# An attention-then-MLP kernel on one core: the prologue's u, first cumulative products and zero products rewritten, and the last tile in halves

## The chip, the core and the metric

The kernel runs on one core of a Trainium2 chip. The time is device time in microseconds (us) of one execution, from outside the span; the profiled span is from the first to the last instruction. TensorE is called PE (its weight loads PEld), VectorE DVE, ScalarE ACT, GpSimd POOL and SyncE SP. SPq and ACTq are the queues from which SP and ACT issue DMAs. Every engine takes its instructions in the order in which the program gives them.

## What is computed

A linear attention with a decaying state, for 4 batches of 8 heads, 768 steps and 48 dimensions, then an MLP with a leaky ReLU over the 3072 rows of 384:

```python
state = 0
for t in range(S):
    cur = u * k[t] (outer) v[t]
    y[t] = r[t] @ (state + cur)
    state = w[t] * state + k[t] (outer) v[t]
x = y, heads side by side            # 3072 x 384
h = x @ w_in                         # 384 x 2048
out = max(0.01 * h, h) @ w_out       # 2048 x 384
```

All inputs and the output are float32; the matrix products run in bf16 with float32 accumulation.

## The kernel before

**Attention by chunks.** The 3072 rows are 24 chunks of 128 steps (6 for each batch). In a chunk the decay is brought into r and k by cumulative sums of log w, so that the chunk needs only matrix products. The steps of chunk i, with engine and line:

- log of w (ACT, L254; for the first four chunks in pairs, L258);
- cum, cumulative sums of the logs by a product with a triangle of ones, and their column sums (PE, L282 and L284; for chunks 0 to 3 L268 and L274, and a second product cum2 at L293 in place of DVE's neg, L300);
- exp and exn, exponentials of the sums and their negatives (ACT, L307 and L310);
- kr = k and r times these (DVE, L314);
- trans, the transposes of kr (PE, L346) and a copy to rkT (ACT L351 or DVE L353); from chunk 10 on a DMA transpose from SP's queue instead (L357);
- scores "at" (PE, L367), two masks (DVE, L375), the mix "y" of state and scores with v (PE, L386 and L392), the new state: kv (PE, L405), tt (DVE, L413), st (POOL, L423);
- the part of u: t1 = r times u (POOL, L318), t2 = t1 times k (POOL, L322), diag, its sum over a head (DVE, L333), vsc = v times diag (POOL, L337), and ysb = y + vsc (DVE, L400);
- ytr, the transposes of ysb (PE, L433) and the copy into xT (ACT, L441); from chunk 18 on by DMA from SP's queue (L436).

**u.** It is loaded as one row by ACT's queue (L204), spread over 128 partitions by a float32 product with a row of ones (PE, L208) and copied to `ukb` (DVE, L211), which t1 reads.

**MLP by tiles.** The rows are also cut in tiles of 256 or 128 (L446). For a tile PE makes the hidden products "hp" (L462), ACT the leaky ReLU into "gt" (L468), PE the output products "op" (L474), ACT the copy to "osb" (L481), and ACT's queue the store (L485). hp of a tile needs xT of its chunks and the weights `w_in`, op needs gt and `w_out`; the weights come in four quarters each, cast to bf16 by DVE (L239 and L242). gt has two buffers, so hp of tile q waits for op of tile q-2.

**Loads.** All come from SP's queue in one list (L507): chunk 0, 1, 2, `w_in` quarters among chunk 3, chunk 4, then the four quarters of `w_out`, then the other chunks.

**Order.** Class Order plans the program ahead: every step has an engine, an assumed duration, what it needs, what PSUM buffers it takes (pool "att" has 5, pool "mlp" 3) and a rank. Again and again it takes the step that can start first by the plan; at equal times the one with the lower rank, which is the chunk's number plus an offset from OFF (L495), or above 100 for MLP products. A DMA that waits for a result (transposes, in the same SP queue as the loads) is taken ahead of a load only if the plan has it ready earlier by SLACK (L497). The program is emitted in that order. While the planned time is under WARM (L494), gaps of PE in the plan are filled with products of zeros (L609), of 512 columns, as many as the planned gap holds.

Of the kernel before, what the change touches and what calls it, by code (L numbers as in the profile page):

```python
# [15 lines left out]
class Order:  # L16
# [20 lines left out]
    def run(self, pools):  # L37
        ends, out = {}, []
        self.times = []
        free = {}  # L40
        slots = {p: [None] * n for p, n in pools.items()}
        place = {}
        todo = {}
# [64 lines left out]
def kernel(  # L108
# [47 lines left out]
    lwp_b = [const.tile([128, 2, H, 64], BF16, name=f"lwp{i}") for i in range(EARLY // 2)]  # L156
    one_row = const.tile([1, 128], F32, name="one_row")
    u_row = const.tile([1, DM], F32, name="u_row")
    kr_b = [const.tile([128, 2 * H, 64], BF16, name=f"kr{i}") for i in range(NB3)]
# [6 lines left out]
    def constants():  # L166
        for t, x, op in ((tri2, 1.0, ALU.is_gt), (trin2, -1.0, ALU.is_ge)):
            nc.gpsimd.memset(t[:], x)
            nc.gpsimd.affine_select(
                out=t[:], in_=t[:], compare_op=op, fill=0.0, base=0, pattern=[[-1, 2], [1, 256]],  # L170
                channel_multiplier=-2,
            )
        nc.gpsimd.memset(tri[:], 1.0)
        nc.gpsimd.affine_select(
            out=tri[:], in_=tri[:], compare_op=ALU.is_gt, fill=0.0, base=0,
            pattern=[[1, 128]], channel_multiplier=-1,
        )
        make_identity(nc, ident)
        nc.vector.memset(ones[:], 1.0)
        nc.vector.memset(idle[:], 0.0)  # L180
        nc.vector.memset(one_row[:], 1.0)
        for t in lwp_b:
            nc.vector.memset(t[:, :, :, D:64], 0.0)
        for t in kr_b + lw_b:
            nc.vector.memset(t[:, :, D:64], 0.0)
        for t in st_b:
            nc.vector.memset(t[:], 0.0)
# [15 lines left out]
    def load_u():  # L203
        nc.scalar.dma_start(out=u_row[:], in_=u.rearrange("h d -> (h d)").rearrange("(a n) -> a n", a=1))  # L204

    def spread_u():
        ub = stage["u"] = ps_att.tile([128, DM], F32, name="ub", tag="att")
        nc.tensor.matmul(ub[:], lhsT=one_row[:], rhs=u_row[:], start=True, stop=True)  # L208

# [53 lines left out]
    def a_cum(i):  # L263
        if i < EARLY:
            r0, m = 64 * (i % 2), i // 2
            cum = att[i]["cum"] = ps_att.tile([128, 512], F32, name="cum", tag="att")
            for j in range(2):
                nc.tensor.matmul(  # L268
                    cum[:, 0:DM], lhsT=tri2[r0 : r0 + 64, j, 2 * r0 : 2 * r0 + 128],
                    rhs=lwp_b[m][r0 : r0 + 64, j, :, 0:D], start=(j == 0), stop=False, skip_group_check=True,  # L270
                )
            for p in range(NP):
                for j in range(2):
                    nc.tensor.matmul(  # L274
                        cum[:, DM + p : DM + p + 1], lhsT=pair(lwp_b[m][r0 : r0 + 64, j], p),
                        rhs=ones[r0 : r0 + 64, :], start=False, stop=(p == NP - 1 and j == 1),
                        skip_group_check=True,
                    )
# [3 lines left out]
        nc.tensor.matmul(cum[:, 0:DM], lhsT=tri[:], rhs=lw[:, :, 0:D], start=True, stop=False, skip_group_check=True)  # L282
        for p in range(NP):
            nc.tensor.matmul(  # L284
                cum[:, DM + p : DM + p + 1], lhsT=pair(lw, p), rhs=ones[:], start=False, stop=(p == NP - 1),
                skip_group_check=True,
            )

    def a_cum2(i):
        cum2 = att[i]["neg"] = ps_mlp.tile([128, H, D], F32, name="cum2", tag="mlp")  # L290
        r0, m = 64 * (i % 2), i // 2
        for j in range(2):
            nc.tensor.matmul(  # L293
                cum2[:], lhsT=trin2[r0 : r0 + 64, j, 2 * r0 : 2 * r0 + 128],
                rhs=lwp_b[m][r0 : r0 + 64, j, :, 0:D], start=(j == 0), stop=(j == 1),
            )
# [148 lines left out]

    sizes = [256, 256, 128, 128, 128, 128, 256, 256, 256, 128, 256, 128, 256, 256, 256]  # L446
    assert sum(sizes) == B * S
# [30 lines left out]

    def m_copy(q, ts):
        osb = osbs[q, ts] = opool.tile([128, NOUT], F32, name="osb")  # L480
        nc.scalar.copy(out=osb[:], in_=ops.pop((q, ts))[:])  # L481

    def m_store(q, ts):
        row = starts[q] + ts * 128
        nc.scalar.dma_start(out=out[row : row + 128, :], in_=osbs.pop((q, ts))[:])  # L485

# [15 lines left out]
    add("const", "POOL", 3.2, constants, rank=-1)  # L502
    add("u", "ACT", 0.3, load_u, lag=2.4, rank=-3)
    add("ub", "PE", 1.2, spread_u, lag=0.2, rank=-3, needs=["u"], takes=(("att", ("ukb",)),))
    add("ukb", "DVE", 0.5, copy_u, needs=["ub"], rank=-3)
    users = []
    queue = [('in', 0), ('in', 1), ('in', 2), ('w_in', 0), ('in', 3), ('w_in', 1), ('w_in', 2), ('w_in', 3), ('in', 4), ('w_out', 0), ('w_out', 1), ('w_out', 2), ('w_out', 3)] + [("in", i) for i in range(5, NCH)]  # L507
    for kind, n in queue:
        past_user = users[-NIN:][:1] if len(users) >= NIN else []
        if kind == "in":  # L510
            if n < EARLY:
                order.alias(("w", n), ("wp", n // 2))
                if n % 2 == 0:
                    add(("wp", n // 2), "DMA", 1.35, load_wp, n // 2, lag=1.95,
                        needs=[("logp", n // 2 - 1)] if n else [])
                    add(("logp", n // 2), "ACT", 0.86, a_logp, n // 2, needs=[("wp", n // 2)], rank=n)
# [64 lines left out]
    for q, mb in enumerate(sizes):  # L581
# [8 lines left out]
        for ts in range(mb // L):  # L590
            for part in range(NQ):
# [4 lines left out]
            tiles.append((q, ts))  # L596
            add(("copy", q, ts), "ACT", 0.48, m_copy, q, ts, rank=0, needs=[("out", q, ts, NQ - 1)]
                + [("store", *x) for x in tiles[-NOUTB - 1 : -NOUTB]])
            add(("issue", q, ts), "ACT", 0.3, m_store, q, ts, rank=-1, needs=[("copy", q, ts)])
# [43 lines left out]
```

## Time and profile before

| what | value |
|---|---|
| median of 7 runs (lowest, highest) | 187.23 us (186.68, 189.46) |
| the profiled execution: time, span | 187.73 us, 186.0 us |
| PE busy | 176.5 us (95%), 1954 products |
| DVE, ACT, POOL busy | 113.3, 113.0, 109.2 us (59 to 61%) |
| PE hp L462, op L474 busy | 72.1 us, 69.5 us |
| zero products L609 | 22, 7.5 us, all before 17 us |
| moved by DMA | 34.46 MB, 115553 of 120696 packets under 512 B |
| granted PE clock in the record | 1.00 throughout |

The slices of the page cut the span in 40 parts; a digit is the busy share in tenths. The chain of waits follows the work that ended last back from the last instruction, at each step to what released it. A line of the timeline has start and length in us, engine, line, what is written and read, and in brackets how long the engine had been idle and for whom. PE's products are pipelined: the ends are modelled, so that sums of busy time are above the pure streaming time.

### The profile page before, as it was taken

What the parts mean: (1) busy time and instruction counts of PE and PEld (TensorE: products, weight loads), DVE (VectorE), ACT (ScalarE), POOL (GpSimd) and SP (SyncE); (2) the same over time, 40 slices, a digit from 0 to 9 for tenths busy, and PEclk for the clock granted to TensorE, in tenths of its full rate; (3) what the DMA queues carried; (4) which work ended last, traced back from release to release, by engine and by line L of the source; (5) the groups of instructions that cost most, each with busy time, mean ns of one, the idle gap of its engine ahead of it and who ended that gap; (6) DMA issues with size and microseconds to landing.
All of it is one profiled execution on the core that took longest, in us unless ns stands there. A gap on an engine that the chain in (4) does not pass through costs nothing.

```text
span 186.0 us, 4892 instructions
## 1 busy us (share of the span) xinstructions
PE 176.5 (95%) x1954; PEld 134.0 (72%) x1955; DVE 113.3 (61%) x187; ACT 113.0 (61%) x218; POOL 109.2 (59%) x144
## 2 busy tenths in 40 slices
PE   7999767999999999999999999999999999999992
PEld 1365557956878878678796688869785786887961
DVE  4377994296689988838395675857575474460000
ACT  2666657914757857577694468669573465662731
POOL 7579954504666699996748786656558368320000
PEclk9999999999999999999999999999999999999999
DMA  6999899999989999999979999899997989422102
GB/s 134 186 211 276 221 351 175 335 375 165 272 164 230 187 202 185 201 184 225 208 154 176 187 197 207 170 193 201 183 161 155 184 173 216 111 63 64 45 6 79
DMA packets 120696, 34.46 MB, mean 185 GB/s; under 512 B 115553, under 2 KB 118626, under 8 KB 120674
## 3 DMA queue, kind: packets, MB, share of 16 engines
q1 hardware_dynamic: 117216, 29.43, 81.8%
q10 hardware_dynamic: 3458, 4.72, 7.5%
q8 instruction: 15, 0.25, 0.6%
q14 instruction: 7, 0.06, 0.1%
HBM read 25.17 MB, written 4.72 MB: 161 GB/s over the span
## 4 chain that ended last, share of the span: by engine, by line
PE 73%; SPq 11%; DMA 9%; DVE 2%; ACT 2%; issue 1%; ACTq 0%; DVEq 0%
PE op L474 33%; PE hp L462 26%; SPq L201 9%; DMA ws<-in_moe_w_out_dram 4%; PE at L367 3%; DMA rkT<-kr 3%; SPq L225 2%; DMA wp<-in_w_dram 2%; PE y L392 2%; PE cum L282 2%; PE trp L346 2%; PE ytr L433 2%; PE y L386 1%; PE kv L405 1%; PE cum L284 1%
## 5 line engine op out<-in xcount | busy, mean ns | idle before, releaser
L462 PE MATMUL hp<-xT,w_in_b 128*128 128x256 bf16 (+1 forms) x720 | 72.1, 252 | 0.5 <-ACT xT L441 0.2
L474 PE MATMUL op<-w_out_b,gt 128*128 128x384 bf16 x384 | 69.5, 326 | 0.3 <-DVE w_out_b L242 0.3
L468 ACT ACTIVATE gt<-hp 128x512 bf16<-128x512 f32 x96 | 56.7, 596 | 21.1 <-PE hp L462 17.5
L462 PEld LDWEIGHTS <-w_in_b 128*128 128x128 bf16 x720 | 62.8, 114 | 3.9 <-DVE w_in_b L239 0.9
L474 PEld LDWEIGHTS <-gt 128*128 128x128 bf16 x384 | 35.6, 98 | 20.6 <-DVE w_out_b L242 0.5
L318 POOL TENSOR_TENSOR t<-in,ukb 128x384 f32<-128x384 f32 x24 | 24.2, 1009 | 22.7 <-DMA in<-in_r_dram 22.4
L375 DVE TENSOR_TENSOR mt<-at,tri 128x512 bf16<-128x512 f32 x48 | 30.9, 684 | 9.8 <-PE at L367 9.6
L314 DVE TENSOR_TENSOR kr<-e,in 128x768 bf16<-128x768 f32 x24 | 27.3, 1139 | 10.9 <-ACT e L310 9.7
L423 POOL TENSOR_TENSOR st<-tt,e 48x192 bf16<-48x192 f32 x40 | 22.6, 565 | 14.1 <-DVE tt L413 10.3
L337 POOL TENSOR_TENSOR vsc<-in,diag 128x384 f32<-128x384 f32 x24 | 22.7, 946 | 11.0 <-DVE diag L333 10.5
L322 POOL TENSOR_TENSOR t<-t,in 128x384 f32<-128x384 f32 x24 | 26.0, 1082 | 2.1 <-DMA in<-in_k_dram 0.8
L400 DVE TENSOR_TENSOR ysb<-y,vsc 128x384 bf16<-128x384 f32 x24 | 13.3, 552 | 11.9 <-PE y L392 8.0
L307 ACT ACTIVATE e<-cum 128x388 f32<-128x388 f32 x24 | 11.9, 494 | 13.7 <-PE cum L284 5.4
L481 ACT COPY osb<-op 128x384 f32<-128x384 f32 x24 | 11.4, 476 | 14.2 <-PE op L474 14.0
L300 DVE SCALAR_TENSOR_TENSOR neg<-cum,lw 128x384 f32<-128x384 f32 x20 | 11.1, 553 | 9.9 <-ACT e L307 9.7
L333 DVE TENSOR_REDUCE diag<-t 128x8 f32<-128x384 f32 x24 | 13.1, 545 | 5.2 <-POOL t L322 5.2
L329 POOL CAST vb<-in 128x384 bf16<-128x384 f32 x20 | 12.3, 616 | 5.4 <-DMA in<-in_v_dram 3.7
L254 ACT ACTIVATE lw<-in 128x384 bf16<-128x384 f32 x20 | 10.4, 520 | 8.1 <-DMA in<-in_w_dram 8.1
L310 ACT ACTIVATE e<-neg 128x384 f32<-128x384 f32 x20 | 10.4, 522 | 4.4 <-DVE neg L300 2.6
L441 ACT COPY xT<-ytr 128x384 bf16<-128x384 bf16 x18 | 8.6, 477 | 2.1 <-ACT osb L481 1.2
L367 PE MATMUL at<-rkT 48*128 48x128 bf16 x192 | 9.5, 219 | 0.3 <-DMA rkT<-kr 0.3
L413 DVE TENSOR_TENSOR tt<-kv,st 128x384 f32<-128x384 f32 x16 | 8.8, 550 | 0.9 <-PE kv L405 0.6
(55 smaller groups left out, 135.9 us busy)
## 6 DMA issues: line engine op xcount, KB each, us to landing
in<-in_r_dram SPq DMA_DIRECT2D x24, 192.0 KB, 4.6
in<-in_k_dram SPq DMA_DIRECT2D x24, 192.0 KB, 4.8
in<-in_v_dram SPq DMA_DIRECT2D x24, 192.0 KB, 4.8
out_dram<-osb ACTq DMA_DIRECT2D x24, 192.0 KB, 3.1
in<-in_w_dram SPq DMA_DIRECT2D x20, 192.0 KB, 4.6
ws<-in_moe_w_in_dram SPq DMA_DIRECT2D x4, 768.0 KB, 6.5
ws<-in_moe_w_out_dram SPq DMA_DIRECT2D x4, 768.0 KB, 7.2
wp<-in_w_dram SPq DMA_DIRECT2D x2, 384.0 KB, 4.4
```

Of the source, the lines that this page charges most:

```text
L201: nc.sync.dma_start(out=ins[i][name], in_=src[b, :, c * L : (c + 1) * L, :].rearrange("h p d -> p h d"))
L314: nc.vector.tensor_tensor(out=kr_b[i % NB3][:, :, 0:D], in0=e, in1=ins[i]["kr"], op=ALU.mult)
L318: nc.gpsimd.tensor_tensor(out=t1[:], in0=flat(ins[i]["r"]), in1=ukb[:], op=ALU.mult)
L322: nc.gpsimd.tensor_tensor(out=flat(t2[:]), in0=att[i]["t1"][:], in1=flat(ins[i]["k"]), op=ALU.mult)
L337: nc.gpsimd.tensor_tensor(out=vsc[:], in0=ins[i]["v"], in1=att[i]["diag"][:].unsqueeze(2).to_broadcast([128, H, D]), op=ALU.mult,)
L367: nc.tensor.matmul(ats[x][:, p, :], lhsT=rkT[r0 : r0 + D, 0, p, :], rhs=rkT[r0 : r0 + D, 1, p, :], start=True, stop=True,)
L375: nc.vector.tensor_tensor(out=att[i]["mt"][:, x], in0=att[i]["ats"][x][:], in1=tri[:].unsqueeze(1).to_broadcast([128, NP, 128]), op=ALU.mult,)
L400: nc.vector.tensor_tensor(out=ysb[:], in0=att[i]["y"][:], in1=flat(att[i]["vsc"][:]), op=ALU.add)
L423: nc.gpsimd.tensor_tensor(out=sn[r0 : r0 + D, :, x * D : (x + 1) * D], in0=tt[r0 : r0 + D, :, x * D : (x + 1) * D], in1=el[r0 : r0 + D, :] ...
L462: nc.tensor.matmul(hp[:, jj, :], lhsT=w_in_b[:, wq, t, f0::JQ], rhs=xT[:, t, t0 : t0 + mb], start=(t == 0), stop=(t == KT - 1),)
L468: nc.scalar.activation(out=gts[q][:, j : j + nj, :], in_=hps.pop((q, j))[:], func=AF.Prelu, alpha=0.01)
L474: nc.tensor.matmul(ops[q, ts][:], lhsT=gts[q][:, j, ts * 128 : (ts + 1) * 128], rhs=w_out_b[:, j, :], start=(j == 0), stop=(j == NFT - 1),)
```

## The change

1. u: POOL clears `u_row` of 65 partitions, ACT's queue loads u into rows 0, 32 and 64, and DVE splits it by five instructions (split_u) into three bf16 parts that add up to u. One bf16 product with ones over 65 rows spreads their sum (spread_u).
2. cum and cum2 of chunks 0 to 3 use all 128 rows of the pair; the rows of the other chunk meet zeros in the triangle tables (two memsets on POOL) and in `ones2`.
3. Zero products fill PE's planned gaps up to planned time 33, kept by two steps of an engine "CLOCK"; they have 256 columns and lie in pool "att", of which one buffer is reserved until then.
4. The last tile of 128 rows is copied and stored in two halves: columns 0 to 191 by ACT and ACT's queue, the others by DVE and SP's queue.
5. Tiles: two of 128 rows become one of 256, 14 instead of 15. OFF, SLACK and some assumed durations have new values; DVE's memset of the zero operand comes first.

```diff
@@ Order.run
+        slots["att"][0] = "warm"
@@ constants
             for t, x, op in ((tri2, 1.0, ALU.is_gt), (trin2, -1.0, ALU.is_ge)):
...
+            nc.gpsimd.memset(t[0:64, :, 128:256], 0.0)
...
+        nc.vector.memset(idle[:], 0.0)
         nc.vector.memset(ones[:], 1.0)
-        nc.vector.memset(idle[:], 0.0)
         nc.vector.memset(one_row[:], 1.0)
+        nc.vector.memset(ones2[:], 0.0)
+        nc.vector.memset(ones2[0:64, 0:1], 1.0)
+        nc.vector.memset(ones2[64:128, 1:2], 1.0)
@@ load_u, split_u, spread_u
-        nc.scalar.dma_start(out=u_row[:], in_=u.rearrange("h d -> (h d)").rearrange("(a n) -> a n", a=1))
+        nc.gpsimd.memset(u_row[:], 0.0)
+        for r0 in (0, 32, 64):
+            nc.scalar.dma_start(
+                out=u_row[r0 : r0 + 1, :], in_=u.rearrange("h d -> (h d)").rearrange("(a n) -> a n", a=1)
+            )
+
+    def split_u():
+        nc.vector.tensor_copy(out=u_part[:], in_=u_row[:])
+        nc.vector.tensor_tensor(out=u_rest[0:33, :], in0=u_row[0:33, :], in1=u_part[0:33, :], op=ALU.subtract)
+        nc.vector.tensor_copy(out=u_part[0:33, :], in_=u_rest[0:33, :])
+        nc.vector.tensor_tensor(out=u_rest[0:1, :], in0=u_rest[0:1, :], in1=u_part[0:1, :], op=ALU.subtract)
+        nc.vector.tensor_copy(out=u_part[0:1, :], in_=u_rest[0:1, :])
...
-        nc.tensor.matmul(ub[:], lhsT=one_row[:], rhs=u_row[:], start=True, stop=True)
+        nc.tensor.matmul(ub[:], lhsT=one_row[:], rhs=u_part[:], start=True, stop=True)
@@ a_cum (a_cum2 likewise)
-                    cum[:, 0:DM], lhsT=tri2[r0 : r0 + 64, j, 2 * r0 : 2 * r0 + 128],
-                    rhs=lwp_b[m][r0 : r0 + 64, j, :, 0:D], start=(j == 0), stop=False, skip_group_check=True,
+                    cum[:, 0:DM], lhsT=tri2[:, j, 128 * n : 128 * n + 128], rhs=lwp_b[m][:, j, :, 0:D],
+                    start=(j == 0), stop=False, skip_group_check=True,
...
-                        cum[:, DM + p : DM + p + 1], lhsT=pair(lwp_b[m][r0 : r0 + 64, j], p),
-                        rhs=ones[r0 : r0 + 64, :], start=False, stop=(p == NP - 1 and j == 1),
-                        skip_group_check=True,
+                        cum[:, DM + p : DM + p + 1], lhsT=pair(lwp_b[m][:, j], p), rhs=ones2[:, n : n + 1],
+                        start=False, stop=(p == NP - 1 and j == 1), skip_group_check=True,
@@ tiles, last tile
-    sizes = [256, 256, 128, 128, 128, 128, 256, 256, 256, 128, 256, 128, 256, 256, 256]
+    sizes = [256, 256, 128, 128, 128, 128, 256, 256, 256, 256, 256, 256, 256, 256]
...
+    HALF = NOUT // 2
+
+    def m_copy(q, ts, last):
         osb = osbs[q, ts] = opool.tile([128, NOUT], F32, name="osb")
...
+        n = HALF if last else NOUT
+        nc.scalar.copy(out=osb[:, 0:n], in_=ops[q, ts][:, 0:n])
...
+    def m_copy2(q, ts):
+        osb = osbs["last"] = opool.tile([128, HALF], F32, name="osb2", bufs=1)
+        nc.vector.tensor_copy(out=osb[:], in_=ops[q, ts][:, HALF:])
+
+    def m_store2(q, ts):
+        row = starts[q] + ts * 128
+        nc.sync.dma_start(out=out[row : row + 128, HALF:], in_=osbs["last"][:])
@@ the plan
-    WARM = 18.0
-    OFF = {'exn': -1.5, 'log': -1.5, 'trans': -2.5, 'ytr': -0.5, 'exp': -2.5, 'scores': -0.5, 't2': 1.5, 't1': -2.5, 'ysb': 1.5, 'vb': 1.5, 'vsc': 1.5}
+    WARM = 33.0
+    COLD = 8.2
+    OFF = {'exn': -1.5, 'log': -1.5, 'ytr': -0.5, 't1': -2.5, 'ysb': 1.5, 'm1': 1.5, 'trans': 2.5, 'cum': 2.5, 'kr': 0.5, 'st': 0.5, 'scores': 0.5, 't2': 2.5, 'm0': 1.5, 'neg': -0.5, 'exp': -1.5, 'vb': 2.5, 'vsc': -0.5}
...
-    SLACK = 1.2
+    SLACK = 0.4
...
-    add("u", "ACT", 0.3, load_u, lag=2.4, rank=-3)
-    add("ub", "PE", 1.2, spread_u, lag=0.2, rank=-3, needs=["u"], takes=(("att", ("ukb",)),))
+    add("u", "ACT", 0.5, load_u, lag=2.6, rank=-3)
+    add("split", "DVE", 2.1, split_u, rank=-3, needs=["u"])
+    add("ub", "PE", 0.25, spread_u, lag=0.2, rank=0.5, needs=["split"], takes=(("att", ("ukb",)),))
...
+    warm = []
+    add("cold", "CLOCK", WARM, warm.append, 0)
+    add("warm", "CLOCK", 0.01, warm.append, 1, needs=["cold"])
...
-        scratch = ps_mlp.tile([128, 512], F32, name="scratch", tag="mlp")
+        scratch = ps_att.tile([128, 512], F32, name="scratch", tag="att")
...
-            if eng == "PE" and at < WARM:
-                for _ in range(int((start - at) / (0.45 if at < 6.0 else 0.22))):
-                    nc.tensor.matmul(scratch[:], lhsT=idle[:, 0:128], rhs=idle[:], start=True, stop=True)
+            if eng == "PE" and len(warm) < 2:
+                for _ in range(int((start - at) / (0.22 if at < COLD else 0.11))):
+                    nc.tensor.matmul(scratch[:, 0:256], lhsT=idle[:, 0:128], rhs=idle[:, 0:256], start=True, stop=True)
```

More of the change, by code (lines that the diff above doesn't have):

```diff
@@ L156 @@
     lwp_b = [const.tile([128, 2, H, 64], BF16, name=f"lwp{i}") for i in range(EARLY // 2)]
-    one_row = const.tile([1, 128], F32, name="one_row")
-    u_row = const.tile([1, DM], F32, name="u_row")
+    ones2 = const.tile([128, 2], BF16, name="ones2")
+    u_row = const.tile([65, DM], F32, name="u_row")
+    u_rest = const.tile([65, DM], F32, name="u_rest")
+    u_part = const.tile([65, DM], BF16, name="u_part")
+    one_row = const.tile([65, 128], BF16, name="one_row")
     kr_b = [const.tile([128, 2 * H, 64], BF16, name=f"kr{i}") for i in range(NB3)]
@@ L264, in a_cum @@
         if i < EARLY:
-            r0, m = 64 * (i % 2), i // 2
+            n, m = i % 2, i // 2
             cum = att[i]["cum"] = ps_att.tile([128, 512], F32, name="cum", tag="att")
@@ L290, in a_cum2 @@
         cum2 = att[i]["neg"] = ps_mlp.tile([128, H, D], F32, name="cum2", tag="mlp")
-        r0, m = 64 * (i % 2), i // 2
+        n, m = i % 2, i // 2
         for j in range(2):
             nc.tensor.matmul(
-                cum2[:], lhsT=trin2[r0 : r0 + 64, j, 2 * r0 : 2 * r0 + 128],
-                rhs=lwp_b[m][r0 : r0 + 64, j, :, 0:D], start=(j == 0), stop=(j == 1),
+                cum2[:], lhsT=trin2[:, j, 128 * n : 128 * n + 128], rhs=lwp_b[m][:, j, :, 0:D],
+                start=(j == 0), stop=(j == 1),
             )
@@ L477, in m_out, with m_store @@
             )
-    def m_copy(q, ts):
+    HALF = NOUT // 2
+    def m_copy(q, ts, last):
         osb = osbs[q, ts] = opool.tile([128, NOUT], F32, name="osb")
-        nc.scalar.copy(out=osb[:], in_=ops.pop((q, ts))[:])
-    def m_store(q, ts):
+        n = HALF if last else NOUT
+        nc.scalar.copy(out=osb[:, 0:n], in_=ops[q, ts][:, 0:n])
+    def m_store(q, ts, last):
         row = starts[q] + ts * 128
-        nc.scalar.dma_start(out=out[row : row + 128, :], in_=osbs.pop((q, ts))[:])
+        n = HALF if last else NOUT
+        nc.scalar.dma_start(out=out[row : row + 128, 0:n], in_=osbs[q, ts][:, 0:n])
+    def m_copy2(q, ts):
[4 more added lines that the diff above has]
+        nc.sync.dma_start(out=out[row : row + 128, HALF:], in_=osbs["last"][:])
     def m_stored(q, ts):
@@ L513 @@
                 if n % 2 == 0:
-                    add(("wp", n // 2), "DMA", 1.35, load_wp, n // 2, lag=1.95,
+                    add(("wp", n // 2), "DMA", 1.35, load_wp, n // 2, lag=1.95 if n else 2.4,
                         needs=[("logp", n // 2 - 1)] if n else [])
@@ L596 @@
             tiles.append((q, ts))
-            add(("copy", q, ts), "ACT", 0.48, m_copy, q, ts, rank=0, needs=[("out", q, ts, NQ - 1)]
+            last = starts[q] + (ts + 1) * 128 == B * S
+            if last:
+                add(("copy2", q, ts), "DVE", 0.28, m_copy2, q, ts, rank=200, needs=[("out", q, ts, NQ - 1)])
+                add(("store2", q, ts), "DMA", 0.4, m_store2, q, ts, lag=1.9, rank=200, needs=[("copy2", q, ts)])
+            add(("copy", q, ts), "ACT", 0.28 if last else 0.48, m_copy, q, ts, last, rank=0, needs=[("out", q, ts, NQ - 1)]
                 + [("store", *x) for x in tiles[-NOUTB - 1 : -NOUTB]])
-            add(("issue", q, ts), "ACT", 0.3, m_store, q, ts, rank=-1, needs=[("copy", q, ts)])
+            add(("issue", q, ts), "ACT", 0.3, m_store, q, ts, last, rank=-1, needs=[("copy", q, ts)])
             add(("store", q, ts), "DMA", 0.6, m_stored, q, ts, lag=1.9, rank=-1, needs=[("issue", q, ts)])
+    warm = []
+    add("cold", "CLOCK", WARM, warm.append, 0)
+    add("warm", "CLOCK", 0.01, warm.append, 1, needs=["cold"])
     steps = order.run({"att": 5, "mlp": 3})
```

## The prediction

> **What bounds the kernel now.** I read the slices first, then the chain of work that ended last, in order of time, then the waits of PE and of SP's queue, and last each engine's timeline in the prologue. A change of more or less than 1% (1.87 us on 187.23) is about what a measurement of this kernel can tell from none.
>
> The slices (40 of 4.65 us) show two stages:
>
> ```profile
> PE   7999767999999999999999999999999999999992
> DVE  4377994296689988838395675857575474460000
> DMA  6999899999989999999979999899997989422102
> ```
>
> PE has gaps up to about 30 us and none after. The chain, start and length in us, shows where the stages meet and what closes the first one:
>
> ```profile
> 24.70 3.52 SPq L201
> 28.27 0.82 SPq L201
> 29.14 7.22 DMA ws<-in_moe_w_out_dram
> 36.38 0.97 DVE w_out_b L242
> 37.40 0.82 PE op L474 x4
> ...
> 177.26 5.21 PE op L474 x32
> 182.50 0.48 ACT osb L481
> ```
>
> Up to 29.14 us the chain is mostly SP's queue issuing loads (L201, L225), then the first quarter of `moe_w_out` in flight, its cast, and the first output product at 37.40. From there it is PE. The table of stages gives PE 144.67 us busy of the 145.10 between 37.40 and 182.50; the waits of PE name one there, 0.3 us, for a DMA transpose. So the time is a sum of three: **37.40** (loads up to `moe_w_out`), **145.10** (PE's remaining work, back to back), **3.5** (182.50 to 186.0: last copy, issue, landing). An edit gains only if it brings forward that landing, takes PE work out of the second term, or shortens the tail.
>
> How close PE is to being ready at 37.40 is in its timeline (start, length, [idle before]):
>
> ```profile
> 28.80 0.33 PE L433 MATMUL ytr<-ident,ysb 128*128 128x128 bf16 x3
> 30.16 0.32 PE L282 MATMUL cum<-lw,tri 128*128 128x384 bf16 x1 [1.03 <-ACT lw L254]
> 30.32 0.24 PE L284 MATMUL cum<-ones,lw 128*128 128x1 bf16 x4
> 30.42 6.72 PE L462 MATMUL hp<-xT,w_in_b 128*128 128x256 bf16 x60
> 37.40 0.82 PE L474 MATMUL op<-w_out_b,gt 128*128 128x384 bf16 x4 [0.26 <-DVE w_out_b L242]
> ```
>
> Sixty hidden products end at 37.14, 0.26 before the cast that the output waits for. Two limits nearly coincide: a later chunk 3 delays the end after 0.26 us, an earlier one gains nothing of itself, since the load holds 37.40. It only makes room to do chunk 4's attention before 37.40.
>
> **What the Trainium skill says.** "TensorE: Matmul & The Clock Gate", Part 1: The HAM clock gate: the array runs at half clock until some 3.4 us of sustained activity. The trace agrees: the zero products (L609, 512 columns) take 634 ns at most, 379 in the median. Eight transposes (L346) take 1.03 us at 9.17 and 0.62 at 11.76. The array is thus warm by about 10 us, and its products from 20 us on have full-speed durations (twelve of 256 columns 1.47, as at 80 us). "DMA: Bandwidth & Descriptors", Issuing engines are not separate DMA queues: several issuers share the 16 engines and save only issue time. The trace shows the engines over 0.9 busy in nearly all slices up to 37 us, so u's two extra 1.5 KB loads cost an issue each, and a half store on SP saves little. "GPSIMD Engine Reference", Key points: POOL shares SBUF interfaces with a two-input DVE instruction. The trace agrees: L322 takes 1.00 us at 6.87 beside an idle DVE, 1.60 at 16.59 under L314.
>
> **The change part by part.**
>
> *u.* Before: one issue (0.53), two passes of the f32 product (842 and 1004 ns, 2.68 to 4.25) and the copy at 4.36 to 4.92. After: POOL clears `u_row` first, 384 elements, 0.4 us by L168's 0.53 for 512. ACT's queue waits for it, then issues three times 0.53: 1.3 to 2.9. Behind those issues stands L258, which starts only at 4.62: hidden by 1.7. Landing some 2 us on, about 4.8 (out stores take 1.9 to 3.8). Then five DVE instructions: three casts at about 0.3 (L239 does 1536 elements in 0.97; 384 are a quarter plus a fixed part), two subtractions at about 0.5 (L300: 0.55), sum 1.9, to 6.7. DVE is idle from 4.92 to 7.72, so they fit. The product of 384 cold columns is 0.4 (L268, cold, two in 0.80), the copy 0.56: `ukb` at about 7.8 instead of 4.92. L318 on POOL, at 5.79 before, comes 2 to 3 us later and with it t2, diag, vsc of chunk 0. Cover: vsc(0) ended at 10.66, ysb(0) wanted it at 13.59, slack 2.9. On the path: 0, up to 0.5 if u lands 0.5 later and kr(0) (7.72) queues behind the copy.
>
> *POOL's constants.* The clear and two memsets (256 elements, about 0.3 each) push `ident` from 4.21 to 5.2; its first reader is at 9.17 and POOL's next work at 5.79. Cost 0. DVE's three small memsets: 0.2, in front of 1.9 idle. Moving `idle` first lets the zero products start 0.06 earlier: 0.
>
> *Full rows.* Same count, same columns; K is 128 instead of 64, and durations follow columns. Gain only if array and gate warm earlier: chunk 0's products from 5.51 to 9.9 are cold (L268 pair 0.80, later 0.49; L346 1.03 against 0.62), together under 1 us for kr(0) and trp(0). That is ahead of a stage in which DVE is 0.8 to 0.9 busy, and behind it stands the `moe_w_out` load. Value on the path: at most room.
>
> *Zero products until planned time 33.* Idle on PE between 18.9 and 37.4 adds up to 0.44+0.24+0.41+1.29+0.20+1.03+0.26 = 3.9 us, so some 30 products of 0.11 us. The clock is up already: gain 0. Cost: each gap that the planner puts too long delays PE. At 9.17 the transposes start 0.5 us after kr(0) ended (8.68), with zero products in between. Bounds: 0, and about 1.0 less the 0.26 slack; I take 0.2. The zero tile moves from pool "mlp" to "att", so attention has 4 slots until then; at 17 to 19 us y, kv, cum and trp are what is alive, four. Within the 0.2.
>
> *Chunk 4 before 37.40.* Its trp, at, y, kv and ytr stand after 37.40: 0.45+0.33+0.37+0.17+0.17 = 1.5 us. xT(3) was copied at 31.04 although its product was at 28.80, because ACT stood at chunk 4's log (waiting for the load w) in order. The new ranks put `cum` later, but `log` keeps 4 - 1.5 and `exp` gets the same, both still ahead of xT(3) at rank 3; only the plan's times can part them. If the hidden products start 1 us earlier, trp and at (0.78) may come before 37.40. k(4) is issued only at 24.70 to 28.22 and exn(4) ran at 35.71 behind L468, so not surely: bounds 0 and 1.5, I take 0.3.
>
> *Two tiles of 128 become one of 256.* The 96 products of 128 columns take 0.056 each (24 in 1.34), 48 of 256 take 0.109: 5.36 against 5.25. With one or two short hand-overs less I take 0.2.
>
> *Ranks, SLACK.* The same PE work in another order: 0 if PE stays fed, else a loss (second rival).
>
> *Tail.* ACT's copy of 192 instead of 384 columns: 0.48 becomes about 0.30; DVE's 192, half of L400's 0.55, is 0.28 beside it. The SP issue is beside ACT's 0.34. The landing (1.9 at its shortest) moves half the bytes each, but together the same: I take 0.05 off. Sum 0.25; bounds -0.1 (copies one after the other on one PSUM tile) and 0.5.
>
> **Sum.** -0.3 (chunk 4) -0.2 (tiles) -0.25 (tail) +0.2 (zero products) = -0.55, against the profiled execution's own 187.73 (span 186.0 and 1.7 around it): 187.2. The median of the runs is 0.5 lower, 187.23, so **186.7**.
>
> **The rivals.**
>
> *All of it arrives* (0.20, time 184.8). Chunk 4 wholly before 37.40 (1.5), tiles 0.2, tail 0.4, and 0.3 of waits inside the second stage: 2.4 less. For: 1.0 us of PE's idle ahead of 37.40 is an ordering fault (ACT and PE at chunk 4). Against: k(4) lands late, L468 fills ACT up to 37 us, and `log` keeps its rank.
>
> *Transposes hold SP's queue and PE runs dry* (0.31, time 190.5). SP's queue is in order. It waited 16.8 us for kr at the transposes L357, eleven times, 3.2 at most, with loads queued behind; POOL waited 22.4 us for the loads of r (waits of SP, then the group of L318):
>
> ```profile
> SPq L357 <- DVE kr L314: 16.8, 11, 3.2
> ```
> ```profile
> L318 POOL TENSOR_TENSOR t<-in,ukb 128x384 f32<-128x384 f32 x24 | 24.2, 1009 | 22.7 <-DMA in<-in_r_dram 22.4
> ```
>
> SLACK from 1.2 to 0.4 lets a transpose go ahead of loads when the plan has kr ready only 0.4 before, so each of 14 may hold the queue 0.8 longer: 11.2 us at most, half of it 5.6. Loads land about 4.7 us after issue, so holds up to that are covered by transfers in flight; 3.2 + 0.8 is just within. At the end y of the last chunk is at 166.62, its xT about 4 later at 170.7, and PE's last hidden products begin near 172.7: 2 us of slack. 5.6 less 2 is 3.6 of PE waiting; less the 0.4 gained at tiles and tail, 3.2, so 190.5. It decides from 2 us of delay on. For: PE's queue is also in order, and the smallest stall of a moved step is never made good. Against: waits of PE in that stage are 0.3 in all, and MLP work of nearly 16 us stands behind the last chunk.
>
> *The zero products or the shorter attention pool eat PE before 37.40* (inside the forecast's case): plus 0.75 at most, 187.7 with nothing of chunk 4 gained.
>
> *The change does nothing on the path*, only tail and tiles: 186.8.
>
> **How the numbers follow.** Forecast (the last two included) 0.49, range of its own 185.5 to 188.6. The range reaches down to 184.8, the full gain, and up to 190.3, most of the second rival; about 0.05 lies below and 0.13 above. Faster by over 1% is the first rival, 0.20; slower by over 1% the second, 0.31; within 1%, 0.49.
>
> **What would show it.** Right: the first output product again near 37.4; chunk 4's trp or at ahead of it; PE's idle after it under 0.5; end of PE to end of span 3.2 to 3.3; `ukb` near 7.8 with ysb(0) no later than 14. Wrong: SP's wait for kr well over 20 us and PE waiting for `at` or `ytr` after 100 us (second rival), or a first output product before 36.5, which would mean that the load was not the limit.

## The result and the profile after

The changed kernel takes 190.46 us (median of 12 runs, 189.7 to 191.17) where the kernel before takes 187.38 beside it: a ratio of 1.016 (95% interval 1.0131 to 1.0188), **slower by 1.6%**. Its profiled execution took 190.43 with a span of 188.7. On the terms of the prediction's sum, read from the two traces (the last term from the start of ACT's last copy to the end of the span):

| | before | after | difference |
|---|---|---|---|
| first output product | 37.40 | 39.86 | +2.46 |
| from there to the last copy | 145.10 | 145.47 | +0.37 |
| from there to the end of the span | 3.50 | 3.37 | -0.13 |

So the loss is in the prologue. The slices of the page, 40 of 4.72 us, show a hole that was not there before:

```profile
PE   7499989999999999999999999999999999998992
DVE  4566889467589999966967674676764465630000
DMA  6999998989899997398998989997977899812002
```

PE's second slice (4.7 to 9.4 us) is 4, before 9. PE's timeline says what stands there, and what follows from it (start, length, in brackets the idle time before and its releaser):

```profile
1.25 4.02 PE L651 MATMUL scratch<-idle 128*128 128x256 bf16 x18 [1.25 <-DVE idle L185]
8.08 0.48 PE L228 MATMUL ub<-u_part,one_row 65*128 65x384 bf16 x1 [2.81 <-DVE u_part L224]
8.35 0.84 PE L288 MATMUL cum<-lwp,tri 128*128 128x384 bf16 x2
...
12.18 1.03 PE L365 MATMUL trp<-ident,kr 128*128 128x128 bf16 x8
...
33.30 6.72 PE L481 MATMUL hp<-xT,w_in_b 128*128 128x256 bf16 x60
39.86 0.81 PE L493 MATMUL op<-w_out_b,gt 128*128 128x384 bf16 x4
```

The product that spreads u waits 2.81 us for the last part of the split, and cum(0), whose logs are ready at 5.37, waits behind it: 8.35 instead of 5.51. PE's timeline before:

```profile
5.51 0.80 PE L268 MATMUL cum<-lwp,tri 64*128 64x384 bf16 x2 [0.22 <-ACT lwp L258]
...
11.76 0.62 PE L346 MATMUL trp<-ident,kr 128*128 128x128 bf16 x8
```

The second line is the transposes of chunk 1, which the first experiment comes back to. The sixty hidden products, which began at 30.42 before, begin at 33.30, and the output follows directly. `w_out` is no longer the limit: DVE casts its first quarter at 36.11 (before 36.38), and the product comes 2.8 us after that cast ended at 37.06.

DVE's timeline shows why the split ends so late:

```profile
5.73 0.36 DVE L220 CAST u_part<-u_row 65x384 bf16<-65x384 f32 x1 [2.71 <-DMA u_row<-in_u_dram]
6.12 0.55 DVE L221 TENSOR_TENSOR u_rest<-u_row,u_part 33x384 f32<-33x384 f32 x1
6.71 0.35 DVE L222 CAST u_part<-u_rest 33x384 bf16<-33x384 f32 x1
7.10 0.55 DVE L223 TENSOR_TENSOR u_rest<-u_rest,u_part 1x384 f32<-1x384 f32 x1
7.68 0.35 DVE L224 CAST u_part<-u_rest 1x384 bf16<-1x384 f32 x1
8.59 0.56 DVE L231 COPY ukb<-ub 128x384 f32<-128x384 f32 x1 [0.57 <-PE ub L228]
```

u is there at 5.7 us; the five instructions take 2.3. The plan in the code has u landed at 3.1 (0.5 + lag 2.6) and split at 5.2, and the logs ready at 5.5 (5.1 in the plan before; the first load of w has a lag of 2.4 now, 1.95 before). So by the plan the product of u can start just before cum(0). On the chip it starts 2.7 us after the logs are ready.

The waits of PE and one of SP's queue (us in total, times, longest), and the group of POOL's t1:

```profile
PE ub L228 <- DVE u_part L224: 2.8, 1, 2.8
PE scratch L651 <- DVE idle L185: 1.3, 1, 1.3
PE hp L481 <- DMA xT<-ysb: 1.0, 2, 0.5
PE hp L481 <- DVE w_in_b L259: 0.7, 1, 0.7
```
```profile
SPq L376 <- DVE kr L333: 25.0, 13, 5.5
```
```profile
L337 POOL TENSOR_TENSOR t<-in,ukb 128x384 f32<-128x384 f32 x24 | 27.1, 1131 | 16.7 <-DMA in<-in_r_dram 12.3
```

SP's queue waits for kr 8 us longer at the transposes (25.0, before 16.8), yet POOL waits 10 us less for r (12.3, before 22.4). In the output stage PE waits twice for an xT by DMA, 1.0 in all (before, 0.3 for an rkT).

### The profile page after: what moved, and what is told of

The parts are those of the page before. It is cut to its first block, busy times and chain, and to the rows that moved or that the text cites. A ratio compares the mean times of both kernels' runs of the same rounds, so it can differ in the third digit from the quotient of the medians.

```text
span 188.7 us, 4948 instructions
## 1 busy us (share of the span) xinstructions
PE 179.6 (95%) x1970; PEld 140.5 (74%) x1970; DVE 117.8 (62%) x196; ACT 112.8 (60%) x218; POOL 112.9 (60%) x147
## 3 DMA queue, kind: packets, MB, share of 16 engines
HBM read 25.17 MB, written 4.72 MB: 158 GB/s over the span
## 4 chain that ended last, share of the span: by engine, by line
PE 78%; POOL 7%; DMA 7%; issue 5%; DVE 2%; SPq 0%; ACT 0%; POOLq 0%
PE hp L481 33%; PE op L493 29%; DMA xT<-ysb 5%; PE at L386 3%; POOL t L337 3%; DMA in<-in_r_dram 2%; POOL t L341 2%; PE y L411 2%; PE cum L301 2%; PE ytr L452 1%; PE trp L365 1%; PE kv L424 1%; PE y L405 1%; POOL vsc L356 1%; POOL st L442 1%
## 5 line engine op out<-in xcount | busy, mean ns | idle before, releaser
L481 PEld LDWEIGHTS <-w_in_b 128*128 128x128 bf16 x672 | 61.8, 114 | 4.7 <-DMA xT<-ysb 1.5
L337 POOL TENSOR_TENSOR t<-in,ukb 128x384 f32<-128x384 f32 x24 | 27.1, 1131 | 16.7 <-DMA in<-in_r_dram 12.3
L333 DVE TENSOR_TENSOR kr<-e,in 128x768 bf16<-128x768 f32 x24 | 28.4, 1185 | 8.9 <-ACT e L329 6.9
L442 POOL TENSOR_TENSOR st<-tt,e 48x192 bf16<-48x192 f32 x40 | 22.1, 552 | 16.4 <-DVE tt L432 10.9
L356 POOL TENSOR_TENSOR vsc<-in,diag 128x384 f32<-128x384 f32 x24 | 23.4, 976 | 13.7 <-DVE diag L352 8.9
L341 POOL TENSOR_TENSOR t<-t,in 128x384 f32<-128x384 f32 x24 | 27.9, 1163 | 5.0 <-DMA in<-in_k_dram 3.7
L503 ACT COPY osb<-op 128x384 f32<-128x384 f32 (+1 forms) x24 | 11.3, 471 | 16.4 <-PE op L493 16.0
L651 PE MATMUL scratch<-idle 128*128 128x256 bf16 x87 | 14.1, 313 | 1.3 <-DVE idle L185 1.3
L651 PEld LDWEIGHTS <-idle 128*128 128x128 bf16 x87 | 9.4, 112 | 3.6 <-DVE idle L185 1.2
```

The lines of the kernel that those rows point to most:

```text
L333: nc.vector.tensor_tensor(out=kr_b[i % NB3][:, :, 0:D], in0=e, in1=ins[i]["kr"], op=ALU.mult)
L337: nc.gpsimd.tensor_tensor(out=t1[:], in0=flat(ins[i]["r"]), in1=ukb[:], op=ALU.mult)
L341: nc.gpsimd.tensor_tensor(out=flat(t2[:]), in0=att[i]["t1"][:], in1=flat(ins[i]["k"]), op=ALU.mult)
L356: nc.gpsimd.tensor_tensor(out=vsc[:], in0=ins[i]["v"], in1=att[i]["diag"][:].unsqueeze(2).to_broadcast([128, H, D]), op=ALU.mult,)
L442: nc.gpsimd.tensor_tensor(out=sn[r0 : r0 + D, :, x * D : (x + 1) * D], in0=tt[r0 : r0 + D, :, x * D : (x + 1) * D], in1=el[r0 : r0 + D, :] ...
L481: nc.tensor.matmul(hp[:, jj, :], lhsT=w_in_b[:, wq, t, f0::JQ], rhs=xT[:, t, t0 : t0 + mb], start=(t == 0), stop=(t == KT - 1),)
```

## The experiments

The theories: **A**, u comes late in queues that are served in order; **B**, the zero products until 33 and the buffer kept for them; **C**, the ranks and SLACK; later **D** and **E** on the output stage and the tail, **F** on the clock. Ratios are to the kernel before, with 95% intervals.

### Only the product of u moved back

```diff
+    late = [x for x in both if x[0] in ((spread_u, ()), (copy_u, ()), (a_t1, (0,)), (a_t2, (0,)))]
+    both = [x for x in both if x not in late]
+    at = next(n for n, x in enumerate(both) if x[0] == (a_cum2, (1,))) + 1
+    both[at:at] = late
```

> The changed kernel with one thing different: the product that spreads u (and its copy, and t1 and t2 of chunk 0 after it) stands behind the cumulative products of chunks 0 and 1 instead of ahead of them. Theory A (PE's queue stands 2.8 us at this product for the split of u, with cum(0) behind it): cum(0) starts near 5.5 us instead of 8.35, the first output product near 37.4 instead of 39.86, span about 186.1, ratio to the kernel before 0.995 to 1.004. Theory B (the zero products until 33 and the attention pool of four make the prologue late): cum(0) is earlier but the first output product stays at 39 or later, ratio 1.012 or more. Theory C (ranks and SLACK starve PE after 100 us): the first output product is early, but PE waits later, ratio above 1.008.

Measured, in four executions: 1.014 (1.0061 to 1.0218). cum(0) starts at 5.49 and kr(0) at 8.15 (10.61 in the changed kernel), as A has it, but the first output product at 40.03. DVE's timeline, then PE's:

```profile
9.03 0.54 DVE L231 COPY ukb<-ub 128x384 f32<-128x384 f32 x1
11.76 0.55 DVE L352 TENSOR_REDUCE diag<-t 128x8 f32<-128x384 f32 x1 [2.19 <-POOL t L341]
12.22 1.26 DVE L333 TENSOR_TENSOR kr<-e,in 128x768 bf16<-128x768 f32 x1
```
```profile
13.54 1.03 PE L365 MATMUL trp<-ident,kr 128*128 128x128 bf16 x8 [2.13 <-DVE kr L333]
14.37 2.71 PE L656 MATMUL scratch<-idle 128*128 128x256 bf16 x12
...
17.02 0.40 PE L386 MATMUL at<-rkT 48*128 48x128 bf16 x8
```

The same three in the changed kernel:

```profile
15.08 0.62 PE L365 MATMUL trp<-ident,kr 128*128 128x128 bf16 x8
15.54 1.47 PE L651 MATMUL scratch<-idle 128*128 128x256 bf16 x12
16.95 0.40 PE L386 MATMUL at<-rkT 48*128 48x128 bf16 x8
```

The wait has moved to the next queue. DVE's program has diag(0) ahead of kr(1); diag needs t2 of POOL, t2 needs t1, t1 needs `ukb` at 9.57. kr(1) stands behind it until 12.22 (12.51 in the changed kernel), and PE's transposes of chunk 1 behind kr(1): they start at 13.54, 1.8 later than before (11.76), though 1.5 earlier than in the changed kernel. That gain is lost again in the profiled execution. After the 2.13 us of idle PE runs at half speed (granted clock 0.50 from 13.49 to 16.89), so that the transposes and the twelve zero products take 1.03 and 2.71 instead of 0.62 and 1.47, and the scores of chunk 1 start at 17.02. The expectation of A failed as it was put: the product ahead of cum(0) is one of two places at which u is late. What the second costs by itself can't be read from this run.

### The new way of u alone

The kernel before, with load_u, split_u, spread_u and their planned durations as in the changed kernel (and its lag of 2.4 for the first load of w, which puts cum(0) behind the product in the plan):

```diff
-    add("u", "ACT", 0.3, load_u, lag=2.4, rank=-3)
-    add("ub", "PE", 1.2, spread_u, lag=0.2, rank=-3, needs=["u"], takes=(("att", ("ukb",)),))
+    add("u", "ACT", 0.5, load_u, lag=2.6, rank=-3)
+    add("split", "DVE", 2.1, split_u, rank=-3, needs=["u"])
+    add("ub", "PE", 0.25, spread_u, lag=0.2, rank=0.5, needs=["split"], takes=(("att", ("ukb",)),))
...
-                    add(("wp", n // 2), "DMA", 1.35, load_wp, n // 2, lag=1.95,
+                    add(("wp", n // 2), "DMA", 1.35, load_wp, n // 2, lag=1.95 if n else 2.4,
```

> The kernel before with only the new way of u (three loads, the split, one bf16 product), planned with the same durations as in the changed kernel, so that its product stands ahead of cum(0). Theory A: cum(0) near 8.3 us, first output product near 39.9, ratio 1.012 to 1.018. Theories B and C: ratio 1.000 to 1.004, because the prologue takes up a later u.

Measured: 1.0111 (1.008 to 1.0142), a little under A's range, and the prologue of the changed kernel. PE's timeline:

```profile
8.23 0.48 PE L221 MATMUL ub<-u_part,one_row 65*128 65x384 bf16 x1 [3.35 <-DVE u_part L217]
8.64 0.82 PE L281 MATMUL cum<-lwp,tri 64*128 64x384 bf16 x2
...
39.67 0.81 PE L487 MATMUL op<-w_out_b,gt 128*128 128x384 bf16 x4
```

With none of the other edits the first output product comes 2.27 us later than before; of the 1.6% u makes 1.1, with the order that its assumed durations bring.

### All but u

The changed kernel with load_u, spread_u, their tiles and planned durations as before.

```diff
-    add("split", "DVE", 2.1, split_u, rank=-3, needs=["u"])
-    add("ub", "PE", 0.25, spread_u, lag=0.2, rank=0.5, needs=["split"], takes=(("att", ("ukb",)),))
+    add("ub", "PE", 1.2, spread_u, lag=0.2, rank=-3, needs=["u"], takes=(("att", ("ukb",)),))
...
```

> The changed kernel with u as it was before (one load, one float32 product of one row); all else as changed. Theory A: ratio 0.995 to 1.004, first output product near 37.4. Theories B and C: ratio above 1.010.

Measured: 1.000 (0.9967 to 1.0033), first output product at 37.81. All the rest of the change together is worth nothing that can be measured. B and C fall as causes of the loss by themselves. The planner gives this run the changed kernel's order of loads and transposes on SP's queue, so that order costs nothing by itself either. (The profile is of an execution of 189.35, above this kernel's median of 187.57, so its later stages are not compared.)

### The zero products as before

```diff
-        slots["att"][0] = "warm"
...
-    WARM = 33.0
+    WARM = 18.0
...
-        scratch = ps_att.tile([128, 512], F32, name="scratch", tag="att")
+        scratch = ps_mlp.tile([128, 512], F32, name="scratch", tag="mlp")
...
-                for _ in range(int((start - at) / (0.22 if at < COLD else 0.11))):
-                    nc.tensor.matmul(scratch[:, 0:256], lhsT=idle[:, 0:128], rhs=idle[:, 0:256], start=True, stop=True)
+                for _ in range(int((start - at) / (0.45 if at < 6.0 else 0.22))):
+                    nc.tensor.matmul(scratch[:], lhsT=idle[:, 0:128], rhs=idle[:], start=True, stop=True)
```

> The changed kernel with the zero products as before (until planned time 18, 512 columns, in the MLP pool, five buffers for attention). Theory A: ratio stays at 1.012 to 1.020. Theory B: ratio 0.998 to 1.005. Theory C: ratio stays at 1.012 or more, like A, but with PE's waits after 100 us.

Measured: 1.0089 (1.0063 to 1.0114), between the two, and clear of the changed kernel's interval. The first output product is at 39.82, as late as with the change, so the prologue is not made late by the zero products. Where u is late they cost 0.7% more, with the order that the planner makes for them, though nothing where u is as before. In the profiled executions the output stage is 144.35 instead of 145.47, without the two waits for xT.

### u planned when it is there

```diff
-    add("u", "ACT", 0.5, load_u, lag=2.6, rank=-3)
-    add("split", "DVE", 2.1, split_u, rank=-3, needs=["u"])
+    add("u", "ACT", 0.5, load_u, lag=5.1, rank=-3)
+    add("split", "DVE", 2.3, split_u, rank=-3, needs=["u"])
```

> The changed kernel with two assumed durations set to what its trace shows: u has landed at 5.6 us instead of 3.1, and the split takes 2.3 instead of 2.1. The planner then puts the product that spreads u behind the cumulative products of chunks 0 and 1 on PE, and diag of chunk 0 behind kr of chunk 1 on DVE. Theory A, widened by the run with only the product moved (there DVE stood 2.2 us at diag(0), with kr(1) behind it): u is late in two queues, and out of both the prologue is as before: kr(1) by 10.5 us, first output product at 37.3 to 38.0, ratio 0.996 to 1.004. Rival (three rows are late whatever the order, since ysb of chunk 0 needs them): first output product above 39, ratio above 1.010.

Measured: 0.9975 (0.9941 to 1.0009). No instruction on u is taken away, only the planner knows when u arrives. DVE's timeline, then PE's:

```profile
7.95 0.94 DVE L333 TENSOR_TENSOR kr<-e,in 128x768 bf16<-128x768 f32 x1
8.82 0.54 DVE L231 COPY ukb<-ub 128x384 f32<-128x384 f32 x1
9.29 0.94 DVE L333 TENSOR_TENSOR kr<-e,in 128x768 bf16<-128x768 f32 x1
11.58 1.29 DVE L394 TENSOR_TENSOR mt<-at,tri 128x512 bf16<-128x512 f32 x2 [1.36 <-PE at L386]
13.03 0.55 DVE L352 TENSOR_REDUCE diag<-t 128x8 f32<-128x384 f32 x1 [0.16 <-POOL t L341]
```
```profile
5.56 0.48 PE L288 MATMUL cum<-lwp,tri 128*128 128x384 bf16 x2 [0.41 <-ACT lwp L278]
...
8.07 0.32 PE L228 MATMUL ub<-u_part,one_row 65*128 65x384 bf16 x1 [0.65 <-DVE u_part L224]
...
37.37 0.81 PE L493 MATMUL op<-w_out_b,gt 128*128 128x384 bf16 x4
```

`ukb` is at 9.4, later than in the changed kernel (9.15), and the first output product is at 37.37. So u's lateness itself costs nothing that can be measured; what stood behind it did. Two things bound this. The planner orders later steps anew as well: diag(0) stands behind kr(1) and behind the masks of chunk 0 too. And PE is at full speed from the first cumulative products on (0.48 at 5.56; before, 0.80 at 5.51). SP's queue waits 24.1 us for kr at its transposes here too, with no loss, and POOL waits 12.3 us for r as in the changed kernel.

The same kernel once more:

> The run with u planned late once more, for the interval: if it beats the kernel before, the ratio's interval lies below 1 (0.994 to 0.999); if not, it holds 1.

Measured: 1.0016 (0.9976 to 1.0056). It is level with the kernel before, not better. (Its profile is of an execution of 190.02, above the median of 188.25, and is not compared.)

### The other parts, with u out of the way

Three runs with the same edits combined: u and zero products both as before; u planned late and zero products as before; u, OFF and SLACK as before.

```diff
-    OFF = {'exn': -1.5, 'log': -1.5, 'ytr': -0.5, ...
-    SLACK = 0.4
+    OFF = {'exn': -1.5, 'log': -1.5, 'trans': -2.5, ...
+    SLACK = 1.2
```

> The changed kernel with u as before and the zero products as before; full rows, ranks, SLACK, tiles and halves remain. The run with old zero products alone had its output stage (first output product to the end of PE) at 144.3 us, the changed kernel 145.4. Theory D (the reserved buffer and the longer filling order the output stage worse by about 1 us): first output product near 37.5, ratio 0.992 to 0.997. Rival (that stage is shorter only because a late prologue leaves time to put other work before it): ratio 0.998 to 1.003.

> The run with u planned late and, besides, the zero products as before. Theories A and D together: ratio 0.992 to 0.998. Theory A without D: 0.998 to 1.004. Neither: above 1.008.

> The changed kernel with u as before, and OFF and SLACK as before; zero products until 33, full rows, tiles and halves remain. Against the run with u as before alone (ratio 1.000): theory C (the new ranks and SLACK cost time after 100 us): ratio 0.990 to 0.996. If they are worth nothing: 0.998 to 1.003. If they gain: above 1.004.

Measured: 1.0031 (0.9984 to 1.0078), 1.0043 (1.0 to 1.0085), 0.998 (0.9947 to 1.0013). D falls: with u out of the way the old zero products aren't better, and C has nothing left to explain. In the second of these the output begins at 36.69 and its stage lasts 145.40; in the last it begins at 38.84 and lasts 143.82. The two terms of the sum trade against each other: in the last, the transposes and scores of chunk 4 stand ahead of the first output product (35.32 and 37.17), and PE need not do them after it. In the first the output begins at 36.46 and its stage lasts 147.90, which is no such trade: PE waits there 1.96 us for an rkT by DMA at 164 and then runs at half speed (granted clock 0.50 from 164.36 to 167.76).

### The last tile in two PSUM tiles

The run with u planned late, with one more edit:

```diff
+                for x in ("a", "b"):
+                    ops[x] = ps_mlp.tile([128, NOUT // 2], F32, name="op" + x, tag="mlp")
...
+                    nc.tensor.matmul(
+                        ops[x][:], lhsT=gts[q][:, j, ts * 128 : (ts + 1) * 128],
+                        rhs=w_out_b[:, j, n * HALF : (n + 1) * HALF], start=(j == 0), stop=(j == NFT - 1),
+                    )
...
-        nc.vector.tensor_copy(out=osb[:], in_=ops[q, ts][:, HALF:])
+        nc.vector.tensor_copy(out=osb[:], in_=ops["b"][:])
...
```

> The run with u planned late, and the last tile's output products in two PSUM tiles of 192 columns, one for each half. In the changed kernel DVE's copy of its half waited for ACT's copy of the other half of the same tile (185.68 after 185.33), so that the second store was issued 0.38 later. Theory E (the halves gain nothing because the two copies of one PSUM tile follow each other): with two tiles both copies start together, and from the end of PE to the end of the span it takes 3.0 to 3.1 us instead of 3.4; ratio to the kernel before 0.993 to 0.998. Rival (the tail is set by the landing alone): 3.4 as before, ratio as in the run with u planned late (0.9975).

Measured: 1.002 (0.9987 to 1.0053). The ends of the timelines of ACT and DVE, in the changed kernel and in this run:

```profile
185.33 0.32 ACT L503 COPY osb<-op 128x192 f32<-128x192 f32 x1 [2.12 <-PE op L493]
185.68 0.36 DVE L513 COPY osb<-op 128x192 f32<-128x192 f32 x1 [16.12 <-ACT osb L503]
186.06 0.36 SPq L517 DMA_DIRECT2D out_dram<-osb  x1
```
```profile
183.25 0.32 ACT L515 COPY osb<-opa 128x192 f32<-128x192 f32 x1 [2.08 <-PE opa L497]
183.33 0.36 DVE L525 COPY osb<-opb 128x192 f32<-128x192 f32 x1 [15.95 <-PE opb L497]
183.72 0.36 SPq L529 DMA_DIRECT2D out_dram<-osb  x1
```

With one tile DVE's copy waits for ACT's, with two they run side by side, as E has it. But the tail shrinks only from 3.37 to 3.25, less than expected and far under what a median shows, and the ratio is not in E's range; what sets the rest of the tail stays open.

### Half rows again

The run with u planned late, with cum and cum2 of chunks 0 to 3 as in the kernel before:

```diff
-                    cum[:, 0:DM], lhsT=tri2[:, j, 128 * n : 128 * n + 128], rhs=lwp_b[m][:, j, :, 0:D],
+                    cum[:, 0:DM], lhsT=tri2[r0 : r0 + 64, j, 2 * r0 : 2 * r0 + 128],
+                    rhs=lwp_b[m][r0 : r0 + 64, j, :, 0:D], start=(j == 0), stop=False, skip_group_check=True,
...
```

> The run with u planned late, with cum and cum2 of the first four chunks over 64 rows again. There the first pair of cumulative products took 0.48 us at 5.56, so the array was at full speed 4 us earlier than in the kernel before (0.80 at 5.51). Theory F (it is full speed because zero products of all rows run without a break from 1.25 to 5.15; full rows in cum add nothing): the pair takes 0.48 to 0.50, ratio 0.995 to 1.001. Rival (half rows let the clock fall back or keep it low): pairs of 0.80 up to 9 us, ratio up by 0.002 or more.

Measured: 1.0028 (0.9983 to 1.0073), which doesn't tell the two apart. PE's timeline shows that each has a part of it right:

```profile
5.56 0.48 PE L288 MATMUL cum<-lwp,tri 64*128 64x384 bf16 x2
...
8.35 0.32 PE L228 MATMUL ub<-u_part,one_row 65*128 65x384 bf16 x1 [1.28 <-DVE u_part L224]
...
9.64 1.06 PE L366 MATMUL trp<-ident,kr 128*128 128x128 bf16 x8
...
38.89 0.81 PE L494 MATMUL op<-w_out_b,gt 128*128 128x384 bf16 x4
```

The first pair is at full speed with half rows as with full ones, as F has it. Then the clock falls back, as the rival has it: the granted clock is 0.50 from 8.88 to 12.28, the transposes take 1.06 (0.61 at 9.00 with full rows), and the first output product is at 38.89. Six of the 12 executions have a mean granted clock of 0.988 to 0.991 and take 188.8 to 190.1 us; the other six have 0.997 or more and take 186.8 to 187.7. With full rows (u planned late, both times, and the last tile in two PSUM tiles) none of 48 executions is under 0.996. So full rows do something here: the clock holds. It does not show in the ratios (1.0028, and 1.0016 for the same kernel with full rows, measured beside it), since executions with full rows spread too, from 186.3 to 190.0 us, with no such fall on record. Why the clock holds is not shown; in the 3.4 us before the fall PE was busy for 2.05, with full rows at like times (4.67 to 8.07) for 2.34. That the zero products alone bring the early speed stays open too.

## Why the prediction was wrong

It said 186.7 us, within 1% most likely; measured are 190.46, just above its range (184.8 to 190.3).

- **The step that failed** is u: "On the path: 0, up to 0.5 if u lands 0.5 later and kr(0) (7.72) queues behind the copy." The times in it were near: landing "about 4.8" was 5.7, the five instructions "sum 1.9" took 2.3, `ukb` "at about 7.8" was ready at 9.15: landing and split make up the whole difference. What it left out is whom PE leaves waiting. It followed u forward to vsc and ysb, where there is slack, and asked of DVE's copy what queues behind it (kr(0)), but never of the product on PE. There cum(0) waits behind it, and behind cum(0) the whole prologue: 2.84 us at cum(0), 2.46 at the first output product. The same holds once more on DVE, where kr(1) stands behind diag(0): with only the product moved, the transposes of chunk 1 still came 1.8 us later than before. The first was there to be found: the diff's durations put the end of the split at 0.5 + 2.6 + 2.1 = 5.2, just ahead of the logs at 5.5, and the prediction's own 6.7 for it contradicted that order.
- **The bound** was right: 0.26 us of slack at the first output product "a later chunk 3 delays the end after 0.26 us". 2.84 late at cum(0) came out as 2.46 there.
- **Chunk 4 before 37.40** (-0.3) did not come: trp(4) follows the first four output products (40.51 after 39.86). With u planned late it is the same (38.02 after 37.37). The -0.2 for the two tiles of 128 was not tested by itself.
- **Zero products**: +0.2 with bounds 0 and 0.75 is not contradicted; all but u gives 1.000. With u late there is 0.7% between old and new ones. Whether the reserved buffer or the order that the planner makes of it does that was not separated.
- **Full rows** "at most room": in the changed kernel nothing was seen of them. With u out of the way they do more than the way considered (an array that warms earlier): without them the clock falls back in half of the executions. What that is worth in time the ratios don't show.
- **Tail**: -0.25 was taken, -0.13 measured, and even that isn't the halves': with u alone, whose last tile is undivided, it takes 3.35. The lower bound named the reason, the two copies one after the other.
- **The second rival** had the time (190.5) by luck, with the wrong mechanism. Its own first sign came: SP's queue waited 25.0 us for kr. But it waited 24.1 with u planned late, and that run is level with the kernel before; POOL waited less for r in both (12.3, before 22.4).
- **The third rival** (the zero products eat PE) comes to 187.5 by the prediction's own terms (187.23 - 0.2 - 0.25 + 0.75), not 187.7; nothing hangs on it.

Of the 1.6%, 1.1 is shown to be u (u alone), and all of it goes when u is planned late. The other 0.5 points come with u late and the new zero products together: with u alone or with the old zero products the loss is 1.1 and 0.9, with all but u none. In the traces the output stage is 145.47 against 144.68 and 144.35. But single executions of u planned late and of the last tile in two PSUM tiles, which have the same order of steps, differ by more than that there (144.54 and 145.89), so where the 0.5 points are lost is not shown.

## What to carry to other kernels

When an edit makes an operand later, look first at what is queued behind its first reader on that reader's engine, then behind the next reader on its engine, before following the operand to where it is needed: on engines that work in order an early place in the queue for a late operand makes all that stands behind it wait (2.81 us on PE here). In a program ordered by assumed durations, one assumed landing 2.6 us too early can be enough; here two numbers in the plan gave back all that was lost. And undo the suspected edit by itself as well as doing it alone: together the two runs settled what neither the two medians nor the share of busy time showed. Read small differences of a stage from more than one execution.

## What the runs showed of the hardware

- Three loads of 1.5 KB, issued one after the other from 1.25 to 2.36 us, were there at 5.7, 3.3 us after the last issue; the single one before was there by 2.7, at most 1.3 after its issue ended. The loads of w, r and k were in flight in both.
- DVE's small instructions did not get cheaper with fewer partitions: the subtraction of 384 columns took 0.55 us on 33 rows and on 1, the cast 0.35 us on 33 and 1 and 0.36 on 65.
- The clock of PE rises at different times for like work. In the four runs with u planned late and the new zero products (all rows, from 1.25 to about 5.0 us or later) the first cumulative pair is at full speed at 5.6 (0.48 us). With only the product of u moved back, and zero products from 1.25 to 5.48, that pair takes 0.80 at 5.49 and the next 0.49 at 6.80. Where the one-row float32 product stands among the zero products, full speed comes later: a pair of 0.67 at 6.98 and one of 0.48 at 7.69 (u and zero products as before), 0.80 at 8.08 and transposes of 0.61 at 9.72 (u, OFF and SLACK as before), and in the kernel before transposes of 1.03 still at 9.17. So neither full rows nor the one-row product is shown to set it. The Trainium skill ("TensorE: Matmul & The Clock Gate", Part 1: The HAM clock gate) gives some 3.4 us of activity, in windows that do not start with the kernel. The runs with u planned late or its product moved back, at full speed some 4 to 6 us after their first zero product, agree. The kernel before, at half speed 7.9 us after its first, does not: the prediction's "The trace agrees" holds for the half speed and not for the time.
- It also falls back after less idle time than the same section gives, an idle window of some 3.4 us. Full speed was lost after waits of 2.13 us (only the product of u moved: transposes of 1.03 at 13.54, 0.62 at 9.15), 1.96 (u and zero products as before, at 164) and 1.28 (half rows), while after one of 0.65 (u planned late) it stayed. Each of the three falls lasts 3.4 us in the record of granted clock, at 0.50. That record shows these falls (a 7 in the fourth slice of the first run) and none of the slow starts.
